# Attention beside a feed-forward network: values multiplied in bursts of four to six key tiles, with some scores copied from PSUM to SBUF

## The chip, the cores and the metric

The kernel runs on one core of one Trainium2 chip. The metric is device time in microseconds of one execution. The kernel before takes 1437.24 us (median of three runs, 1437.2 to 1437.76). TensorE multiplies matrices, ScalarE applies functions, VectorE does elementwise work and copies, GpSimd does some elementwise work and issues transfers, SyncE issues transfers. Matmul results go to PSUM, which has eight banks of 512 float32 columns over 128 partitions; everything else lies in SBUF.

## The reference

```python
def _A_ref(x, wqkv, wo):                     # 2048 tokens, D = 512, 32 heads of 16
    qkv = (x @ wqkv).reshape(B, S, 3, H, Dh) # then (2, 0, 3, 1, 4)
    q, k, v = qkv[0], qkv[1], qkv[2]
    scores = jnp.einsum("bhqd,bhkd->bhqk", q, k) * Dh ** -0.5
    o = jnp.einsum("bhqk,bhkd->bhqd", softmax(scores), v)
    return o.transpose(0, 2, 1, 3).reshape(B, S, D) @ wo

def _B_ref(x, w_gate, w_up, w_down):         # F = 1792
    return (silu(x @ w_gate) * (x @ w_up)) @ w_down

xn = layernorm(A_x)
out = A_x + _A_ref(xn, wqkv, wo) * silu(_B_ref(xn, w_gate, w_up, w_down))
```

All inputs and the output are float32. There is no causal mask: each query meets all 2048 keys.

## The kernel before

**Stages.** A first stage, to about 160 us, normalises the tokens, projects queries, keys and values, and writes them to DRAM, split in a high and a low part of a reduced float32 (each product is made of three: high by high, high by low, low by high). A second, long stage computes attention and mixes the feed-forward network into it, matmul by matmul, on TensorE. A short end projects the last block of queries.

**Attention.** A unit is a group of four heads and a block of 512 queries: `units` = 32, numbered group by group, four blocks `b` to a group `g`. The keys of a unit are 16 key tiles of 128. For each key tile the four heads' scores are four matmuls (`score<-qst,kst`, L811) with 50 contraction rows each; two heads lie on the lower and two on the upper half of the array's rows (`HALF` = 64), so that two heads' scores run side by side. A pair `j` of heads fills `score[j]`, two PSUM banks; ScalarE takes the exp of both at once into an SBUF tile `pr` (128 x 1024, L813). The values (`acc<-pr,vst`, L356) multiply these probabilities by the four heads' values and a column of ones, each head on its own 32 columns of the array, accumulating over the 16 key tiles in the bank `acc[u % 2]`. `finish` then transposes the accumulator on VectorE, divides by the sum of the probabilities, and, at every second group, transposes once more and stores the result to `o_d`.

**Steps.** A step is two key tiles, so there are 256 (`steps` = 8 to a unit). In each, TensorE runs the scores of the first key tile, the values of the step before (`values(prev)`), the scores of the second tile, and then a share of feed-forward matmuls. The two accumulators let a unit's values start while the previous one is being read.

**Feed-forward.** `ffn(b)` is a generator that yields after each pair of matmuls. A pair is two matmuls with 64 contraction rows each, on the two halves of the array's rows, into `bankx` and `banky` (`both`, L174). For each of the 14 tiles of 128 hidden columns there are 24 pairs for gate and up; ScalarE's tanh (L203) and two steps on VectorE make the gated tile, and `split_hidden` and `split_wd` split it and its rows of `w_down` into two parts (`hh`, `wd`). The hidden tiles are in two groups of `GROUPS`, eight and six; after a group, each of the four token tiles takes 3 pairs a hidden tile for the product with `w_down`. The weights of the next tile are split on VectorE by `split_gu` (L134, L135) when a tile begins. After the feed-forward, `project_out` projects the attention's output for the finished blocks of queries.

**Order.** The order on every engine is that of the program text. `plan` lists how many pairs each step takes, `fill` draws them from the generators, `catch_up` runs what was deferred, `out_steps` loads and splits the parts for the output projection as steps pass. SyncE issues most loads in that order, GpSimd stores `o_d`, `g_d` and the output.

**PSUM.** `bankx` and `banky`, two accumulators `acc`, and two score tiles of two banks each: eight banks.

Of the kernel before, what the change touches and what calls it, by code (L numbers as in the profile page):

```python
# [9 lines left out]
F32 = mybir.dt.float32  # L10
# [9 lines left out]
P = 128  # L20
S = 2048
D = 512
H = 32
DH = 16
# [8 lines left out]
GROUPS = (slice(0, 8), slice(8, NF))  # L33
FG = 8
# [7 lines left out]
FIRST = (4, 5, 2, 2)  # L42
HALVED = 2
EARLY = 2
EPS = 1e-5
QSLOT = (0, 1, 0)
# [4 lines left out]
def tile_block(ctx: ExitStack, tc: tile.TileContext, x, wqkv, wo, w_gate, w_up, w_down, out):  # L51
# [78 lines left out]
    def split_gu(i):  # L130
        raw = gu[i][0]
        hi = two.tile([P, DC, P], F32R, tag="guh", name="guh")
        lo = two.tile([P, DC, P], F32R, tag="gul", name="gul")
        dve.tensor_copy(hi, raw)  # L134
        dve.tensor_sub(lo, raw, hi.bitcast(F32))  # L135
        gu[i] = (hi, lo)

# [33 lines left out]

    def both(lhs, rhs, start, stop):
        for bank, h in zip(banks, halves):
            mm(bank, lhs[h], rhs[h], start=start, stop=stop)  # L174
# [8 lines left out]
    def ffn(b):  # L183
        for grp, part in enumerate(GROUPS):
            nf = part.stop - part.start
            for f in range(nf):
                i = b * NF + part.start + f
                if i + 1 < NB * NF:
                    split_gu(i + 1)
# [4 lines left out]
                for c in range(DC):  # L194
                    for wt, j in ((hi, 0), (hi, 1), (lo, 0)):
                        both(wt[:, c], fx[:, j, c], n == 0, n == 3 * DC - 1)
                        n += 1
                        if n == DC and i:
                            load_wd(i)
# [80 lines left out]
    def load_gates(t):  # L280
        gt[t] = (hh, wd)[t % NT // 2].rearrange("p f j t -> p (f j) t")[:, 14 + t % 2].bitcast(F32)
        xr[t] = plain[t % NT]
        sp.dma_start(gt[t], g_d[rows[t]])
        sp.dma_start(xr[t], x[rows[t]])

    stage = {}
    ready = [0] * NB
    splits = []

    def out_steps():  # L290
        for b in range(NB - 1):
            if b not in stage and (len(queue) <= NB, 0 in stage and now > stage.get(0, now), ready[0] == DT)[b]:
                for c in range(DT - 1):
                    load_out(b, c)
                stage[b] = now
            if b in stage and b < 2 and (b, 1) not in stage and now > (u0 + b) * steps:
                load_out(b, DT - 1)
                stage[b, 1] = now
            if b in stage and (b, 2) not in stage and now > stage[b] and (b < 2 or len(queue) <= 2):
                splits.extend((b, c) for c in range(DT - 1))  # L300
                stage[b, 2] = now
                for t in range(0 if b else NT):
                    load_gates(t)
            if (b, 1) in stage and (b, 5) not in stage and now > stage[b, 1]:
                splits.insert(0 if not b else len(splits), (b, DT - 1))
                stage[b, 5] = now
        for _ in range(min(2, len(splits))):
            b, c = splits.pop(0)
            split_o(lhs[b, c], parts_o[b, c])
            ready[b] += 1  # L310

    def store_out(t, y):
        pool.tensor_mul(y, y, gt[t])
        pool.tensor_add(xr[t], y, xr[t])
        (pool if t < end - 1 else sp).dma_start(out[rows[t]], xr[t])
# [34 lines left out]
    def values(item):  # L350
        u, kp, probs = item
        v, a = vst[(u // NB * NB + kp * 2 // CT) % RING], acc[u % 2]
        for i in range(2):
            kt = 2 * kp + i
            for h in range(4):
                mm(a[h * 32:h * 32 + DH + 1], v[:, kt % CT, h * (DH + 1):(h + 1) * (DH + 1)],  # L356
                   probs[2 * i + h // 2][:, h % 2], start=kt == 0, stop=kt == KT - 1, skip_group_check=True)

    def normalise(u, first, last, between=None):
# [3 lines left out]
        dve.transpose(o1[:, :n], acc[u % 2][:, first:last])  # L363
# [8 lines left out]
    def finish(u):  # L372
        g, b = divmod(u, NB)
        normalise(u, 0, TB)
        if g % 2:
            o2 = late.tile([P, TB], F32, tag="o2", name="o2")
            dve.transpose(o2, on[b])  # L377
            if g < NG - 1 or b < 2:
                (pool if g < NG - 1 else sp).dma_start(o_d[g // 2, b], o2)  # L379
            else:  # L380
                whole = hh.rearrange("p f j t -> p (f j) t")
# [6 lines left out]
    steps = KT // 2  # L388

    u0 = units - NB + 1  # L390

# [19 lines left out]


    shares = []

    def plan():
        def tile_of(n, parts):
            shares.extend([n // parts] * parts)

        halved = 0
        for i in range(2 * NB):  # L420
            nf = GROUPS[i % 2].stop - GROUPS[i % 2].start
            for f in range(nf - (i == 0)):
                tile_of(3 * DC, 3 if i or f else 2)
            for t in range(NT):
                if nf == FG:
                    halved += HALVED
                    tile_of(3 * nf, 3 - halved // (NB * NT))
                    halved %= NB * NT
                else:
                    tile_of(3 * nf, 2)  # L430
        for _ in range(EARLY):
            tile_of(3 * (DT - 1), 1)
        for _ in range(NB * NT - NT):
            tile_of(3 * DT, 1)
        shares[0] += 2 - sum(FIRST[:3])
        shares[1] -= 2 + FIRST[3]

# [3 lines left out]
    def share():  # L441
        if not blocked() and shares:
            fill(shares.pop(0))


    with ExitStack() as pro:
# [211 lines left out]
        for b in range(NB):  # L658
# [3 lines left out]
            for n, (make, i) in enumerate(slots):  # L662
# [11 lines left out]
                if not more and n == 2:  # L674
                    split_gu(0)
# [100 lines left out]
    ppool = ctx.enter_context(tc.tile_pool(name="ppool", bufs=6))  # L776
# [5 lines left out]
    score = [spool.tile([P, 2, 512], F32, name=f"score{i}") for i in range(2)]  # L782
    ring(2, RING, att)
# [9 lines left out]
    plan()  # L793
    prev = None

    exps = []
    for u in range(units):
        g, b = divmod(u, NB)
        q = qst[u % 2]
        for kp in range(steps):  # L800
            now = u * steps + kp
            probs = []
            for i in range(2):
                kt = 2 * kp + i
                k, kc = kst[(g * NB + kt // CT) % RING], kt % CT
                if now == i == 0:
                    fill(FIRST[0])
                for j in range(2):
                    for h in range(2):
                        r = slice(h * HALF, h * HALF + NROW)  # L810
                        mm(score[j][:, h], k[r, j, kc * P:(kc + 1) * P], q[r, j], start=True, stop=True)  # L811
                    pr = ppool.tile([P, 2, TB], F32, tag="pr", name="pr")
                    exps.append(act(pr, score[j], AF.Exp, scale=0.25))  # L813
                    if i == 0 and j == 1 and now:
                        tc.add_manual_dep(exps[-1].ins, exps[-3].ins.name, settled, reason="order of the slots' writes")
                    probs.append(pr)
                    if now == i == 0 and j:
                        fill(FIRST[1])
                    elif (now, i, j) in ((0, 1, 0), (1, 0, 0)):
                        fill(FIRST[2 + now])  # L820
                if i == 0:
                    catch_up()
                if i == 0 and prev:
                    values(prev)
            old, prev = prev, (u, kp, probs)
            share()
            if old and old[1] == steps - 1:
                after.append(partial(finish, old[0]))
            if kp == 0:
                if u + 1 < units:  # L830
# [89 lines left out]
```

## Time and profile before

| | us |
|---|---|
| median of three runs | 1437.24 |
| lowest and highest run | 1437.2, 1437.76 |
| span of the profiled execution | 1435.2 |
| TensorE busy | 1427.3 (99%) |
| ScalarE busy | 1111.2 (77%) |
| VectorE busy | 537.9 (37%) |
| GpSimd busy | 90.9 (6%) |

The span runs from the first to the last instruction of one profiled execution; the median of the runs is 2.0 us above it. The page cuts the span into 40 slices and gives the busy tenths of each engine, and the clock that TensorE was granted. Its chain of waits follows the work that ended last back from the end, naming at each step the engine and line. Its groups list, for each line, engine and operation, the written and read tiles, the shapes and count, then the time in which any of them ran, the mean duration of one in nanoseconds, and the idle time of the engine before them with what ended it. A timeline gives start, duration, engine, line, operation and tiles; `PEld` is TensorE's loading of weights, DVE is VectorE, ACT ScalarE and POOL GpSimd. Matmuls overlap in the array, so their pace is read from one start to the next and not from a duration.

### The profile page before, as it was taken

The numbers are of one execution on the slowest core, as the hardware profiler recorded it, in microseconds if no ns is written. First come the engines' busy times: TensorE is split into PE (matmuls) and PEld (weight loads), VectorE is DVE, ScalarE is ACT, GpSimd is POOL, SyncE is SP. The second block draws the span as 40 slices with busy tenths as digits, with TensorE's granted clock in tenths as the row PEclk, the third lists the DMA queues.
The fourth block names the chain that finished last, engine by engine and source line by source line (L and its number), as shares of the span: only waits on it lengthen the run. The fifth ranks groups of instructions, "written<-read, shape, count | busy, mean of one in ns | idle before, by whom it ended". The sixth has DMA issues, their size and how long they took to land.

```text
span 1435.2 us, 26816 instructions
## 1 busy us (share of the span) xinstructions
PE 1427.3 (99%) x11227; PEld 804.0 (56%) x11227; DVE 537.9 (37%) x899; ACT 1111.2 (77%) x1235; POOL 90.9 (6%) x104
## 2 busy tenths in 40 slices
PE   9999999999999999999999999999999999999998
PEld 7778655555555555555555555555555555555555
DVE  6543344112523343134323441243244422243665
ACT  6733688888888888778888888888888887888764
POOL 4200200000000000000000000000000000000154
PEclk9999999999999999999999999999999999999999
DMA  7778652032264321142553320342835210312553
GB/s 222 264 246 248 160 116 63 19 90 65 67 149 120 96 65 34 39 105 71 112 132 90 95 48 12 79 106 55 177 79 123 63 42 12 101 30 78 196 183 104
DMA packets 127524, 149.15 MB, mean 104 GB/s; under 512 B 12588, under 2 KB 79404, under 8 KB 126628
## 3 DMA queue, kind: packets, MB, share of 16 engines
q1 hardware_dynamic: 122196, 126.84, 34.5%
q0 software_dynamic: 4912, 20.12, 3.8%
q8 instruction: 91, 1.49, 0.5%
q10 hardware_dynamic: 288, 0.39, 0.1%
q14 instruction: 37, 0.30, 0.1%
HBM read 107.20 MB, written 40.11 MB: 103 GB/s over the span
## 4 chain that ended last, share of the span: by engine, by line
PE 89%; DVE 0%; DVEq 0%; issue 0%
PE acc L356 33%; PE bankx L174 31%; PE score L811 20%; PE banky L174 3%; PE acc L858 0%; PE banky L858 0%; PE score L858 0%; DVE y L865 0%; DVE y L871 0%; DVEq L916 0%
## 5 line engine op out<-in xcount | busy, mean ns | idle before, releaser
L813 ACT ACTIVATE pr<-score 128x1024 f32<-128x1024 f32 x1024 | 993.2, 1023 | 223.2 <-PE score L811 222.5
L356 PE MATMUL acc<-pr,vst 128*17 128x512 f32 x4096 | 489.2, 595 | 0.0
L811 PE MATMUL score<-qst,kst 50*128 50x512 f32 x2048 | 352.3, 421 | 0.0
L811 PEld LDWEIGHTS score<-qst,kst 50*128 50x128 f32 x2048 | 177.2, 184 | 263.8 <-ACT pr L813 227.9
L174 PE MATMUL bankx<-fx,guh 64*128 64x512 f32 x896 | 288.8, 392 | 0.1
L174 PE MATMUL banky<-fx,guh 64*128 64x512 f32 x896 | 288.7, 392 | 0.0
L356 PEld LDWEIGHTS acc<-pr,vst 128*17 128x17 f32 x4096 | 93.9, 96 | 234.4 <-issue 233.6
L204 DVE SCALAR_TENSOR_TENSOR ga<-th,bankx 128x512 f32<-128x512 f32 x56 | 38.5, 687 | 446.1 <-ACT th L203 446.1
L174 PEld LDWEIGHTS bankx<-fx,guh 64*128 64x128 f32 x896 | 165.7, 185 | 32.8 <-issue 0.9
L174 PE MATMUL banky<-fx,gul 64*128 64x512 f32 x448 | 175.3, 391 | 0.0
L174 PE MATMUL bankx<-fx,gul 64*128 64x512 f32 x448 | 175.3, 391 | 0.0
L174 PEld LDWEIGHTS banky<-fx,guh 64*128 64x128 f32 x896 | 165.6, 185 | 4.0
L174 PE MATMUL bankx<-wd,hh 64*128 64x512 f32 x672 | 166.7, 389 | 0.0
L174 PE MATMUL banky<-wd,hh 64*128 64x512 f32 x672 | 166.6, 388 | 0.0
L174 PEld LDWEIGHTS bankx<-wd,hh 64*128 64x128 f32 x672 | 124.0, 185 | 26.6
L174 PEld LDWEIGHTS banky<-wd,hh 64*128 64x128 f32 x672 | 124.0, 185 | 1.2
L174 PEld LDWEIGHTS bankx<-fx,gul 64*128 64x128 f32 x448 | 82.8, 185 | 17.0
L174 PEld LDWEIGHTS banky<-fx,gul 64*128 64x128 f32 x448 | 82.8, 185 | 2.0
L569 PE MATMUL ps<-xt,wh 128*128 128x512 f32 x256 | 80.6, 396 | 0.0
L222 DVE COPY facc<-bankx 128x512 f32<-128x512 f32 x16 | 11.1, 691 | 171.5 <-PE banky L174 171.5
L135 DVE TENSOR_TENSOR gul<-gur,guh 128x1024 fp32r<-128x1024 f32 x56 | 68.6, 1225 | 2.4 <-DVE guh L134 0.5
L379 POOL DMA_DIRECT2D o_d<-o x12 | 6.5, 545 | 756.5 <-DVE o L377 563.8
(158 smaller groups left out, 1060.5 us busy)
## 6 DMA issues: line engine op xcount, KB each, us to landing
gur<-in_B_w_gate_dram SPq DMA_DIRECT2D x56, 256.0 KB
gur<-in_B_w_up_dram SPq DMA_DIRECT2D x56, 256.0 KB
wdr<-in_B_w_down_dram SPq DMA_DIRECT2D x56, 256.0 KB
kst<-k_d SPq DMA_DIRECT2D x192, 64.0 KB
qst<-q_d SPq DMA_DIRECT2D x192, 64.0 KB
fx<-xt_d SPq DMA_DIRECT2D x24, 512.0 KB
q_d<-parts SPq DMA_DIRECT2D x16, 512.0 KB
k_d<-parts SPq DMA_DIRECT2D x16, 512.0 KB
```

The costliest lines, as they stand in the source:

```text
L135: dve.tensor_sub(lo, raw, hi.bitcast(F32))
L174: mm(bank, lhs[h], rhs[h], start=start, stop=stop)
L204: dve.scalar_tensor_tensor(ga, th, 1.0, bankx, op0=ALU.add, op1=ALU.mult)
L222: dve.tensor_copy(facc[:, t], bankx)
L356: mm(a[h * 32:h * 32 + DH + 1], v[:, kt % CT, h * (DH + 1):(h + 1) * (DH + 1)], probs[2 * i + h // 2][:, h % 2], start=kt == 0, stop=kt == ...
L379: (pool if g < NG - 1 else sp).dma_start(o_d[g // 2, b], o2)
L569: mm(ps, w, a[:, c], start=n == 0, stop=n == 3 * DT - 1)
L811: mm(score[j][:, h], k[r, j, kc * P:(kc + 1) * P], q[r, j], start=True, stop=True)
L813: exps.append(act(pr, score[j], AF.Exp, scale=0.25))
```

## The change

The unit's 16 key tiles are cut into blocks instead of steps. Most units have three blocks, of five, five and six key tiles (`blocks`, with the six where the feed-forward tile is largest); unit 28 has six, six and four; the units in `FINE` (27, 29, 30, 31) have four blocks of four. There are 100 blocks. Each takes one tile of the feed-forward or of the output projection: the list `sizes` holds 24 pairs for a gate and up tile, 21 for a token tile (both groups now have seven hidden tiles), 9 and 12 for tiles of the output projection. All values of a block follow its scores in one burst.

Only `acc[0]` accumulates; `acc[1]` becomes `spare_bank`. A tile of scores (two heads of one key tile) is taken in one of two ways. A direct one (`D`) goes to a score tile of two banks and through ScalarE's exp, as before. A copied one is written head by head into the spare bank (`A` and `B`), each copied by VectorE into half a `pr` tile, and ScalarE's exp over both halves follows in place after the block's other work. A single head takes one half of the array's rows; the other half goes to a feed-forward matmul, for which the order of the halves is swapped while `lower` is set. `events` lays out the order: how many tiles are direct, and where `D`, `A`, `B` and the pairs `F` stand.

```diff
-GROUPS = (slice(0, 8), slice(8, NF))
-FG = 8
+GROUPS = (slice(0, 7), slice(7, NF))
+FG = 7
...
+PROBS = 11
+FINE = (27, 29, 30, 31)
...
-        dve.tensor_copy(hi, raw)
-        dve.tensor_sub(lo, raw, hi.bitcast(F32))
         gu[i] = (hi, lo)
+        for h in (slice(0, DC // 2), slice(DC // 2, DC)):
+            dve.tensor_copy(hi[:, h], raw[:, h])
+            yield
+            dve.tensor_sub(lo[:, h], raw[:, h], hi[:, h].bitcast(F32))
+            yield
...
+    def order():
+        return (1, 0) if lower else (0, 1)
+
     def both(lhs, rhs, start, stop):
-        for bank, h in zip(banks, halves):
-            mm(bank, lhs[h], rhs[h], start=start, stop=stop)
+        for i in order():
+            mm(banks[i], lhs[halves[i]], rhs[halves[i]], start=start, stop=stop)
...
+                        if n % 4 == 2:
+                            next(pieces, None)
...
+    def out_steps():
+        if now == early:
+            for c in range(DT - 1):
+                load_out(0, c)
+        if now == early + 1:
+            for c in range(DT - 1):
+                load_out(1, c)
+            for t in range(NT):
+                load_gates(t)
...
+    def out_splits():
+        if now in (early, early + 1):
+            split_out(now - early)
+        if now == opened[units - 2] + 1:
+            split_out(2)
...
+    def events(n, f):
+        length = 2 * n + f
+        copied = max(0, 2 * n - max(2, (4 * length - 6) // 16 + 1)) if f else 0
+        direct = 2 * n - copied
+        gap = max(4, min(5, (length - 8) / max(1, direct - 2)))
+        marks = [(0, "D"), (1, "D")] + [(7 + gap * i, "D") for i in range(direct - 2)]
+        marks += [(4 + (length - 6) * i / (2 * copied), "AB"[i % 2]) for i in range(2 * copied)]
...
-    ppool = ctx.enter_context(tc.tile_pool(name="ppool", bufs=6))
+    ppool = ctx.enter_context(tc.tile_pool(name="ppool", bufs=PROBS))
...
+            elif e == "D":
+                kt, j = straight[done]
+                for h in order():
+                    scores(score[done % 2][:, h], kt, j, h)
+                probs[kt, j] = ppool.tile([P, 2, TB], F32, tag="pr", name="pr")
+                act(probs[kt, j], score[done % 2], AF.Exp, scale=0.25)
+                done += 1
+                if done == 2:
+                    while ends:
+                        ends.pop(0)()
+                    out_steps()
+            elif e == "A":
+                kt, j = copies.pop(0)
+                waiting.append((kt, j))
+                scores(spare_bank, kt, j, 0)
+                lower = True
+                probs[kt, j] = ppool.tile([P, 2, TB], F32, tag="pr", name="pr")
+                dve.tensor_copy(probs[kt, j][:, 0], spare_bank)
+            else:
+                kt, j = waiting[-1]
+                scores(spare_bank, kt, j, 1)
+                lower = False
+                dve.tensor_copy(probs[kt, j][:, 1], spare_bank)
+        for kt, j in waiting:
+            act(probs[kt, j], probs[kt, j], AF.Exp, scale=0.25)
+        out_splits()
+        catch_up()
+        values(u, range(first, first + n), probs)
```

The layouts that follow from it, by kind of block (key tiles, pairs: number of blocks, direct tiles, copied tiles):

| block | blocks | direct | copied |
|---|---|---|---|
| 4, 9 | 2 | 4 | 4 |
| 4, 12 | 11 | 5 | 3 |
| 4, 21 | 2 | 7 | 1 |
| 4, 24 | 2 | 8 | 0 |
| 5, 21 | 23 | 8 | 2 |
| 5, 24 | 31 | 9 | 1 |
| 6, 21 | 7 | 8 | 4 |
| 6, 24 | 22 | 9 | 3 |

`finish` of a unit is called after the second direct tile of the next unit's first block. `split_gu` yields between its four operations, and one of them is drawn at every fourth pair. The loads of keys, values, output parts and gates move from steps to blocks. The last twelve pairs of the output projection come after the last values. The scratch for GpSimd's transfers is set to 4096 bytes.

214 lines of the change are left out of this document (99 added, 115 removed).

## The prediction

> **What bounds the kernel now.** I read the page first, then the busy time of the attention stretch, then the timeline of single instructions.
>
> ```profile
> span 1435.2 us, 26816 instructions
> ...
> PE   9999999999999999999999999999999999999998
> ...
> PEclk9999999999999999999999999999999999999999
> ...
> PE acc L356 33%; PE bankx L174 31%; PE score L811 20%; PE banky L174 3%; PE acc L858 0%; PE banky L858 0%; PE score L858 0%; DVE y L865 0%; DVE y L871 0%; DVEq L916 0%
> ...
> L813 ACT ACTIVATE pr<-score 128x1024 f32<-128x1024 f32 x1024 | 993.2, 1023 | 223.2 <-PE score L811 222.5
> L356 PE MATMUL acc<-pr,vst 128*17 128x512 f32 x4096 | 489.2, 595 | 0.0
> L811 PE MATMUL score<-qst,kst 50*128 50x512 f32 x2048 | 352.3, 421 | 0.0
> ...
> L135 DVE TENSOR_TENSOR gul<-gur,guh 128x1024 fp32r<-128x1024 f32 x56 | 68.6, 1225 | 2.4 <-DVE guh L134 0.5
> L222 DVE COPY facc<-bankx 128x512 f32<-128x512 f32 x16 | 11.1, 691 | 171.5 <-PE banky L174 171.5
> ```
> ```profile
> 160.00:1420.00 1260.00, 1260.00 (x10430) 673.86 (x10432) 452.36 (x698) 1028.93 (x1096) 58.79 (x66) 1.00 0.35 87
> ```
>
> The second fence is the stretch 160 to 1420 us: length, then busy time of TensorE, its weight loads, VectorE, ScalarE, GpSimd, and the granted clock, 1.00. TensorE is never idle in it, so the end is set by TensorE's pace alone, and any wait put in front of a matmul is added to the time in full. How much of the pace is lost between kinds of matmul is seen in one step:
>
> ```profile
> 704.22 0.39 PE L174 MATMUL bankx<-wd,hh 64*128 64x512 f32 x1
> ...
> 704.45 0.39 PE L174 MATMUL bankx<-wd,hh 64*128 64x512 f32 x1
> ...
> 706.04 0.63 PE L811 MATMUL score<-qst,kst 50*128 50x512 f32 x4
> 706.50 1.94 ACT L813 ACTIVATE pr<-score 128x1024 f32<-128x1024 f32 x2 [0.64 <-PE score L811]
> ...
> 706.60 1.91 PE L356 MATMUL acc<-pr,vst 128*17 128x512 f32 x16
> 707.04 0.12 PEld L356 LDWEIGHTS acc<-pr,vst 128*17 128x17 f32 x4 [0.31 <-issue]
> 707.47 0.12 PEld L356 LDWEIGHTS acc<-pr,vst 128*17 128x17 f32 x4 [0.31 <-issue]
> ...
> 708.44 0.73 PE L811 MATMUL score<-qst,kst 50*128 50x512 f32 x4
> ...
> 709.00 0.40 PE L174 MATMUL bankx<-wd,hh 64*128 64x512 f32 x1
> ```
>
> A feed-forward pair takes a slot of 0.23 us (704.22 to 704.45), and so should a pair of scores. Four scores (two pairs, 0.46) take 0.56 from 706.04 to 706.60, and 0.56 from 708.44 to 709.00: 0.10 is lost on each side of a values burst. Inside, four quads by 0.43 (707.04 to 707.47) are 1.71, but the burst holds TensorE for 1.84 (706.60 to 708.44): 0.13 more. A burst costs 0.33 us beside its work.
>
> **The change, part by part.** *Fewer bursts.* 4096 records at 16 a burst are 256 bursts. The changed code cuts the 32 units into 28 of three blocks and 4 of four, 100 bursts. The work inside (slots, quads) is the same. 156 x 0.33 = 51 us off. I take it whole; its lower bound is nothing, if the loss came back at the new borders between scores and feed-forward, but runs of 4 scores that border on feed-forward pairs show no loss on that side.
>
> *What ScalarE now paces.* Two exps take 1.94 and one 1.02, so one starts each 0.92 us. Direct tiles are written 4 slots apart, 0.92: no stall, no slack. In a block of five key tiles with 24 pairs, TensorE takes 34 x 0.23 + 0.33 + 10 x 0.43 = 12.4 us, ScalarE 10 x 0.92 + 0.60 = 9.8. Not the bound.
>
> *Scores copied through one bank.* The other tiles' scores go one head at a time into the single bank acc[1], VectorE copies them out, and the next head's matmul waits for that copy, with all TensorE work behind it. The cycle is matmul to copy, copy, copy to matmul:
>
> ```profile
> 710.84 0.39 PE L174 MATMUL banky<-wd,hh 64*128 64x512 f32 x1
> ...
> 711.26 0.69 DVE L226 TENSOR_TENSOR y<-bankx,facc 128x512 f32<-128x512 f32 x1 [5.73 <-PE banky L174]
> ```
> ```profile
> 42.06 0.69 DVE L552 TENSOR_TENSOR xt<-acc,xt 128x512 fp32r<-128x512 f32 x1 [0.54 <-ACT xt L549]
> ...
> 42.80 0.31 PEld L544 LDWEIGHTS acc<-ident,xn 128*128 128x128 f32 x3 [0.56 <-DVE xt L552]
> ```
>
> 0.42 (710.84 to 711.26) + 0.69 (the copy, 691 ns of L222) + 0.05 (42.75 to 42.80) = 1.16. If a weight load must run after the release, its 0.18 makes 1.34. I take 1.22, near the lower end, as the load is pulled ahead elsewhere. The Trainium skill (Perfetto Trace Analysis, Optimizing Tensor Performance) says that independent matmul groups should rotate through several banks, so that one's evacuation overlaps the next's matmuls; one bank goes against it. By that rule the copies would hide with a second bank, and the term below would be nothing; here there is one.
>
> The code spaces a block's copies evenly, whatever VectorE needs. Worked for four key tiles with 12 pairs (six copies, 2.33 slots = 0.54 us apart): the first head is written 1.03 us into the block (four slots and the 0.11 after a burst), the sixth no sooner than 1.03 + 5 x 1.22 = 7.13, and three and a half slots follow: 7.93, against 20 x 0.23 + 0.11 = 4.71 unhindered, so 3.2 us lost. By the same sum:
> - four tiles, 12 pairs: 11 blocks x 3.2 = 35;
> - four tiles, 9 pairs (eight copies): 2 x 6.1 = 12;
> - six tiles, 21 pairs (eight copies, 0.78 apart): 7 x 2.9 = 20;
> - six tiles, 24 pairs (six copies, 1.15 apart, VectorE also splitting weights between them, 1225 / 2 ns a piece against the 0.5 us free per cycle): 22 x 0.65 = 14;
> - five tiles: copies 1.4 us or more apart, nothing.
> Together 81. The gaps between copies are 11 x 5 + 2 x 7 + 7 x 7 + 22 x 5 = 228; 0.06 less or 0.12 more each gives 67 to 108.
>
> *Eleven probability buffers, twelve tiles.* In a block of six the last direct exp takes the buffer of the block's first tile, so it waits for the first quad of the values; the tanh (24 pairs only) and the copied exps queue behind it on ScalarE.
>
> ```profile
> 799.61 0.60 ACT L203 ACTIVATE th<-bankx 128x512 f32<-128x512 f32 x1
> 800.10 1.94 ACT L813 ACTIVATE pr<-score 128x1024 f32<-128x1024 f32 x2
> ```
>
> A tanh holds ScalarE for 0.49 (799.61 to 800.10). Counted from the values' start, with 0.6 for the quad and the handoff: 0.6 + 0.92 + 0.49 + 2 x 0.92 + 1.02 + 0.1 = 5.0 until the last copied exp can be read, and 0.6 + 4 x 0.92 + 1.02 + 0.1 = 5.4 with 21 pairs. The sixth key tile is due after ten quads, 4.3, or its second half after eleven, 4.7; which, the rows do not tell. I take the middle, 0.5 and 0.9: 22 x 0.5 + 7 x 0.9 = 17 us; 0 if other slack exists, 24 with the earlier due time.
>
> *VectorE's queue at a unit's start.* The accumulator's transposition, which was done beside a step, now stands ahead of the block's first copy:
>
> ```profile
> 800.24 0.69 DVE L204 SCALAR_TENSOR_TENSOR ga<-th,bankx 128x512 f32<-128x512 f32 x1 [6.85 <-ACT th L203]
> ...
> 803.28 0.69 DVE L145 TENSOR_TENSOR wd<-wdr,wd 128x512 fp32r<-128x512 f32 x1
> ...
> 814.76 0.69 DVE L204 SCALAR_TENSOR_TENSOR ga<-th,bankx 128x512 f32<-128x512 f32 x1 [8.93 <-ACT th L203]
> ```
> ```profile
> 1382.67 1.65 DVE L262 TENSOR_TENSOR hh<-hh 128x512 fp32r<-128x512 f32 x1
> 1384.25 0.70 DVE L363 STREAM_TRANSPOSE o<-acc 128x512 f32<-128x512 f32 x1
> ...
> 1385.79 0.71 DVE L377 STREAM_TRANSPOSE o<-on 128x512 f32<-128x512 f32 x1
> ...
> 1387.00 0.69 DVE L262 TENSOR_TENSOR hh<-o,hh 128x512 fp32r<-128x512 f32 x1
> ```
>
> It takes 1.5 us (1384.25 to 1385.79), 2.3 with the second transposition, 3.4 with the split for the output projection; and a tile's 3.7 us of gating and splitting (800.24 to 803.97) begins after its tanh and reaches about 1 us into the next block. A block's first copy would start at 1.03 + 0.42 = 1.45; where it starts later and copies are the chain, the difference is lost. Units 30 and 31: 0.3 + 3.4 - 1.45 = 2.3 each. Unit 29, where three splits of an output part also stand in the queue (2 us of them left over): 4.3, and 0.6 in each of two later blocks. Two six-tile blocks at a unit's start: 1.5 each. Five-tile blocks there, five with 21 pairs by about 1.4 and seven with 24 by 0.4: 10. The splits of `wo` and of the last output parts before unit 29: 3.5. About 27 us; 8 to 45, the upper end with L262 at 1.65, as at 1382.67 beside GpSimd.
>
> *The rest.* The tail gains a leftover output tile (12 pairs) after the last values, whose two VectorE steps of 0.69 and 0.42 of latency now stand ahead of the last transposition: 2 us. Exps of copied scores read SBUF; no such exp is shown, nearest is
>
> ```profile
> L645 ACT CAST fx<-xt 64x1024 fp32r<-64x1024 f32 x16 | 16.8, 1048 | 0.3
> DVE wd L144 <- DMA wdr<-in_B_w_down_dram: 10.4, 2, 6.4
> ```
>
> at 1048 against 1023, nothing on the path. The moved loads (keys, gates, output parts on SyncE; stores on GpSimd) are hidden now: VectorE waited for a weight tile twice in all. A tile came each 14.5 us (800.24 to 814.76), it now comes each 12 to 14, so they stay hidden; 0, at most 3. The smaller scratch for GpSimd's transfers has no row: 0 to 2, taken as 0, since TensorE waits for none of them.
>
> Sum: -51 + 81 + 17 + 27 + 2 = +76. On the profiled execution's 1435.2 that is 1511; the runs' median, 1437.24, lies 2.0 above that span, so **1513**.
>
> **The rivals.** *VectorE keeps up* and the copies hide, as the even spacing supposes: 1437 - 51 + 2 = 1388, faster. For it: VectorE was busy 452 of 1260 us, and 428 copies add 296. Against: latency, not load, decides. It holds as soon as the copy cycle is below the spacing, 0.54 us in the last 11 blocks; the rows give 1.16.
>
> *Only the cycle stalls*, in the blocks that have no slack, and buffers and queue cost nothing: 1437 - 51 + 81 + 2 = 1469. For it: the order within a quad and slack on ScalarE are not seen in the trace.
>
> *The switches remain*: the change doesn't remove what it says, the 0.33 reappears where single heads are mixed in, and the stalls come on top: 1513 + 51 = 1564. Against it: pairs on opposite row halves run at 0.23 now.
>
> *The clock falls.* The trace has TensorE at 1.00 and never idle here, so it cannot show what short gaps do. Should the 20 blocks with the densest copies (9, 12 and six tiles with 21 pairs: 11 x 8.3 + 2 x 7.6 + 7 x 12.9, about 200 us of TensorE work by the rows above) run at half clock, a supposition, and half of the loss hide behind the copies, it is 1513 + 100 = 1613. The Trainium skill (TensorE: Matmul & The Clock Gate, A second HAM failure mode: psum-queue depth-cycling) reports such an oscillation where TensorE idles briefly between groups.
>
> *The terms cancel*: 1437, if stalls come to 51.
>
> **How the numbers follow.** Forecast 0.66, VectorE keeps up 0.07, only the cycle 0.13, switches remain 0.08, clock 0.03, cancel 0.03. The likeliest's own range, with each term at its ends, is -51 + 67 + 0 + 8 + 2 = +26 to -51 + 108 + 24 + 45 + 7 = +133, so 1463 to 1570; not all ends come together. For 8 in 10 I take 1455 to 1570. Runs here agree within 0.04%; a change of under 0.2%, 3 us, is none. Faster 0.08 (keeps up, and a little of cancel), same 0.04, slower 0.88.
>
> **What would show it.** TensorE's idle time before scores into acc put down to VectorE's copies, 60 to 110 us, in the blocks of 9, 12 and 21 pairs; starts of such scores 1.2 us apart in the last 110 us; 100 values bursts; waits of values for ScalarE only in six-tile blocks; a last stretch of 13 blocks at about 11.5 us each. I am wrong if heads are written closer than 1.1 us apart, or if feed-forward pairs between them stretch beyond 0.23.

## The result, and the profile after

The changed kernel takes 1583.45 us (median of four runs, 1582.48 to 1586.93) where the kernel before took 1437.33 beside it (1437.2 to 1437.76). The ratio is 1.102, with a 95% interval of 1.1006 to 1.1035. It is slower, as forecast, but by 146 us instead of 76, and the time lies above the forecast range.

These are lines of the page of the changed kernel: span, tenths of TensorE's busy time and of its granted clock in 40 slices, the chain by engine and by line, and groups (line, engine, operation, tiles, shapes, count; busy us and mean ns of one; idle us before them and its end).

```profile
span 1581.4 us, 27925 instructions
...
PE   9999799999999999999999999999999999888887
...
PEclk9999899999999999999999999999999999877978
...
PE 85%; DVE 8%; ACT 4%; issue 2%; DMA 1%; SPq 0%; DVEq 0%; ACTq 0%
PE acc L370 29%; PE bankx L182 18%; PE score L835 12%; PE banky L182 9%; PE acc L835 7%; PE ps L591 5%; ACT pr L846 3%; DVE pr L858 3%; PE ps L593 3%; DVE pr L863 1%; DVE o L377 1%; ACT pr L865 0%; DVE o L391 0%; PE acc L566 0%; DMA v_d<-vt 0%
...
L858 DVE COPY pr<-acc 128x512 f32<-128x512 f32 x214 | 147.6, 690 | 206.0 <-PE acc L835 193.6
...
L835 PE MATMUL acc<-qst,kst 50*128 50x512 f32 x428 | 200.0, 467 | 52.0 <-DVE pr L858 32.8
...
L865 ACT ACTIVATE pr<-pr 128x1024 f32<-128x1024 f32 x214 | 214.5, 1060 | 0.0
```

Before, no engine but TensorE had a share above 0% in the chain of waits. Now VectorE holds 8% of it and ScalarE 4%. TensorE has two weak places, slice 5 and the last six slices, and the granted clock falls in both. L858 and L863 are VectorE's copies of the two heads, 0.69 us each as forecast. Summed by what was waited for (us, times, longest), the weight loads of copied scores and of values, and ScalarE's exps, say whom they waited for:

```profile
PEld acc L835 <- DVE pr L858: 64.8, 77, 3.0
PEld acc L370 <- ACT pr L865: 59.9, 83, 0.8
PEld acc L835 <- DVE pr L863: 46.2, 92, 1.1
```
```profile
ACT pr L846 <- PE acc L370: 56.8, 29, 2.8
```

The copies hold the scores' weight loads back for 111 us (64.8 + 46.2). In 29 cases an exp of direct scores waits for the values: there are exactly 29 blocks of six key tiles, and it is their twelfth probability tile that waits for a buffer. An engine's wait is not yet TensorE's loss, however; for that each block is measured on TensorE. Two blocks of four key tiles and 12 pairs ran at full clock from end to end; one of them has splits of an output part in VectorE's queue ahead of its copies. Here is the other, first TensorE (without the feed-forward matmuls), then VectorE:

```profile
1492.23 0.74 PE L835 MATMUL score<-qst,kst 50*128 50x512 f32 x4
1493.27 0.39 PE L835 MATMUL acc<-qst,kst 50*128 50x512 f32 x1
1494.52 0.49 PE L835 MATMUL acc<-qst,kst 50*128 50x512 f32 x1 [0.38 <-DVE pr L858]
...
1495.80 0.50 PE L835 MATMUL acc<-qst,kst 50*128 50x512 f32 x1 [0.32 <-DVE pr L863]
...
1499.78 0.49 PE L835 MATMUL acc<-qst,kst 50*128 50x512 f32 x1 [0.40 <-DVE pr L858]
1500.91 3.63 PE L370 MATMUL acc<-pr,vst 128*17 128x512 f32 x32
1504.46 0.50 PE L835 MATMUL score<-qst,kst 50*128 50x512 f32 x2
```
```profile
1493.77 0.69 DVE L858 COPY pr<-acc 128x512 f32<-128x512 f32 x1 [3.60 <-PE acc L835]
1495.05 0.69 DVE L863 COPY pr<-acc 128x512 f32<-128x512 f32 x1 [0.59 <-PE acc L835]
1496.40 0.69 DVE L858 COPY pr<-acc 128x512 f32<-128x512 f32 x1 [0.66 <-ACT pr L846]
```

One cycle through the bank: matmul at 1494.52, copy at 1495.05, its end at 1495.74, next matmul at 1495.80, so 0.53 + 0.69 + 0.06 = 1.28 us. Over the block's six heads, from 1493.27 to 1499.78, the mean distance is 1.30. From first score to first value the block takes 1500.91 - 1492.23 = 8.68 us. Its 20 slots of 0.23 and 0.20 for the borders are 4.80, so 3.88 is lost. The 3.55 of the values are the 8 x 0.428 + 0.115 of a burst without waits.

The same subtraction over all 100 blocks, by kind, beside what the prediction gave each place (copies' cycle + VectorE's queue where there are two; its two six-tile blocks at a unit's start are taken as those of units 9 and 20, with 24 pairs):

| place | blocks | forecast, us | measured, us |
|---|---|---|---|
| first two blocks, scores and pairs | 2 | 0, at most 3 | 16.9 |
| six key tiles, values burst | 29 | 17 | 40.0 |
| six key tiles, 21 pairs, scores and pairs | 7 | 20 | 27.5 |
| six key tiles, 24 pairs, scores and pairs | 21 | 14 + 3 | 16.5 |
| five key tiles | 53 | 10 | 15.9 |
| four key tiles, 12 pairs, all | 11 | 35 + 6 | 66.0 |
| four key tiles, 9 pairs, all | 2 | 12 + 8 | 23.3 |
| four key tiles, 21 or 24 pairs | 4 | 0 | 0.7 |
| sum | | 125 | 206.8 |

The attention stretch lasts from 160.1 to 1564.4 us instead of 159.9 to 1422.8, 141.4 more, and the tail 17.0 instead of 12.4, 4.6 more. Together that is the 146. Without the 206.8 the stretch would be 1197.5, 65 less than before, where 51 was forecast. The leftover output tile that moved behind it is 2.8 of these 14; the rest was not separated.

The row nobody had forecast is the first. These are VectorE's operations in block 0, from its timeline, then the scores behind them on TensorE:

```profile
166.15 1.24 DVE L169 CAST hh<-ga 128x512 fp32r<-128x512 f32 x1 [10.28 <-DMA v_d<-vt]
...
170.37 0.69 DVE L858 COPY pr<-acc 128x512 f32<-128x512 f32 x1
...
171.20 0.76 PE L835 MATMUL acc<-qst,kst 50*128 50x512 f32 x1 [5.48 <-DVE pr L858]
```
```profile
187.27 0.43 DVE L147 CAST wd<-wdr 128x512 fp32r<-128x512 f32 x1 [7.22 <-DMA wdr<-in_B_w_down_dram]
...
188.68 0.69 DVE L858 COPY pr<-acc 128x512 f32<-128x512 f32 x1
```

VectorE stands 10.28 us for transfers of the first stage, in block 1 7.22 us for a weight tile. Waits of this length existed before, but no TensorE work depended on what was queued behind them. Now a copy does, and TensorE stands for 5.48 us until it is done.

The clock, in the busy times by stretch (length, then busy us of TensorE, weight loads, VectorE, ScalarE, GpSimd, then the granted clock):

```profile
160.00:190.00 30.00, 18.36 (x129) 12.46 (x131) 12.08 (x19) 13.61 (x15) 6.35 (x6) 0.82 0.67 152
190.00:1369.00 1179.00, 1168.35 (x9385) 677.44 (x9383) 629.93 (x1065) 901.27 (x978) 15.10 (x28) 1.00 0.32 77
1369.00:1564.00 195.00, 165.15 (x919) 69.53 (x916) 100.72 (x151) 101.49 (x104) 35.13 (x33) 0.81 0.22 71
```

In the last stretch the mean is 0.81. The record has only 1.0 and 0.5, so some 195 x 0.19 x 2 = 74 us of it were at half clock.

### The profile page after: what moved, and what is told of

It is laid out like the page before. It is cut to its first block, busy times and chain, and to the rows that moved or that the text cites. A ratio compares the mean times of both kernels' runs of the same rounds, so it can differ in the third digit from the quotient of the medians.

```text
span 1581.4 us, 27925 instructions
## 1 busy us (share of the span) xinstructions
PE 1520.2 (96%) x11227; PEld 890.6 (56%) x11227; DVE 829.0 (52%) x1439; ACT 1098.2 (69%) x1235; POOL 89.4 (6%) x104
## 4 chain that ended last, share of the span: by engine, by line
PE 85%; DVE 8%; ACT 4%; issue 2%; DMA 1%; SPq 0%; DVEq 0%; ACTq 0%
PE acc L370 29%; PE bankx L182 18%; PE score L835 12%; PE banky L182 9%; PE acc L835 7%; PE ps L591 5%; ACT pr L846 3%; DVE pr L858 3%; PE ps L593 3%; DVE pr L863 1%; DVE o L377 1%; ACT pr L865 0%; DVE o L391 0%; PE acc L566 0%; DMA v_d<-vt 0%
## 5 line engine op out<-in xcount | busy, mean ns | idle before, releaser
L846 ACT ACTIVATE pr<-score 128x1024 f32<-128x1024 f32 x810 | 778.7, 1027 | 384.6 <-PE score L835 322.4
L835 PE MATMUL score<-qst,kst 50*128 50x512 f32 x1620 | 411.3, 419 | 0.0
L182 PE MATMUL banky<-fx,guh 64*128 64x512 f32 x896 | 319.8, 399 | 0.0
L182 PE MATMUL bankx<-fx,guh 64*128 64x512 f32 x896 | 312.3, 395 | 0.1
L858 DVE COPY pr<-acc 128x512 f32<-128x512 f32 x214 | 147.6, 690 | 206.0 <-PE acc L835 193.6
L835 PE MATMUL acc<-qst,kst 50*128 50x512 f32 x428 | 200.0, 467 | 52.0 <-DVE pr L858 32.8
L863 DVE COPY pr<-acc 128x512 f32<-128x512 f32 x214 | 148.0, 692 | 139.2 <-PE acc L835 135.4
L865 ACT ACTIVATE pr<-pr 128x1024 f32<-128x1024 f32 x214 | 214.5, 1060 | 0.0
L182 PE MATMUL bankx<-wd,hh 64*128 64x512 f32 x672 | 205.8, 395 | 0.0
L182 PE MATMUL banky<-wd,hh 64*128 64x512 f32 x672 | 196.5, 394 | 0.0
L835 PEld LDWEIGHTS acc<-qst,kst 50*128 50x128 f32 x428 | 81.4, 190 | 131.3 <-DVE pr L858 64.8
```

The source lines that it names most:

```text
L182: mm(banks[i], lhs[halves[i]], rhs[halves[i]], start=start, stop=stop)
L835: mm(bank, k[r, j, kc * P:(kc + 1) * P], q[r, j], start=True, stop=True)
L846: act(probs[kt, j], score[done % 2], AF.Exp, scale=0.25)
L858: dve.tensor_copy(probs[kt, j][:, 0], spare_bank)
L863: dve.tensor_copy(probs[kt, j][:, 1], spare_bank)
L865: act(probs[kt, j], probs[kt, j], AF.Exp, scale=0.25)
```

## The experiments

**One part of the change mended at a time.** Each of the next four runs, and the one with filled gaps, is a single execution; the four of the change spread over 4.4 us. *No copies in the first two blocks:*

```diff
-        copied = max(0, 2 * n - max(2, (4 * length - 6) // 16 + 1)) if f else 0
+        copied = max(0, 2 * n - max(2, (4 * length - 6) // 16 + 1)) if f and now > 1 else 0
```

> The change with no copied scores in its first two blocks (all their tiles go direct); all else as changed. In the changed kernel's trace these two blocks hold their scores and pairs for 8.2 and 8.6 us longer than the unhindered sum, beside VectorE waiting 10.3 and 7.2 us for transfers. Theory (the copies stand behind VectorE's waits for transfers, and TensorE behind the copies): both blocks lose at most 2 us, the clock is 1.00 until the last output tiles; 1583 - 15 = 1568 (1564 to 1572). Rival (the late weights and keys themselves hold TensorE): 1580 to 1586.

1569.45 us, 14 less. VectorE still stands for the same transfer,

```profile
165.41 1.24 DVE L169 CAST hh<-ga 128x512 fp32r<-128x512 f32 x1 [9.78 <-DMA v_d<-vt]
```

but the two blocks lose 1.9 and 2.2 us instead of 8.3 and 8.6, although VectorE's wait for the weight tile grew from 7.2 to 12.4. It is the copy behind the waiting instruction that costs, not the wait.

*Twelve buffers instead of eleven* (room for it from a shared tile and a smaller scratch):

```diff
-PROBS = 11
+PROBS = 12
...
-            o2 = late.tile([P, TB], F32, tag="o2", name="o2")
+            o2 = late.tile([P, TB], F32, tag="o1", name="o2")
...
-dynamic_dma_scratch_size=4096)
+dynamic_dma_scratch_size=2048)
```

> The change with twelve probability buffers instead of eleven (room from half the transfer scratch and one shared late tile). Theory (in blocks of six the last direct exp waits for the first values, and the copied exps queue behind it): the values of those 29 blocks lose their 1.3 to 1.7 us each, 40 us in all; 1583 - 40 = 1543 (1538 to 1552). Rival (ScalarE has too much to do in such a block whatever the buffers): 1575 to 1586, values still 1.0 us or more late.

1546.79 us, 37 less. The bursts of six key tiles lose 0.03 to 0.05 us each, where they lost 1.27 (24 pairs) and 1.72 (21 pairs). ScalarE's 29 waits for the values are gone from the summed waits, and of the values' waits for copied exps there remain

```profile
PEld acc L370 <- ACT pr L865: 17.4, 53, 0.7
```

instead of 59.9. Of these, 13.7 us in 44 waits of at most 0.31 are still in the six-tile blocks with 24 pairs, where they cost nearly nothing (0.03 to 0.05 us a block): a weight load that waits is not yet a matmul that waits. The values of the four-tile blocks of 9 and 12 pairs still lose 12 us.

*A copy of 64 columns instead of 512*, into a scratch tile. The exps of copied scores read the block's first direct probabilities, so copied scores do not enter the output:

```diff
-                dve.tensor_copy(probs[kt, j][:, 0], spare_bank)
+                dve.tensor_copy(short, spare_bank[:, :64])
...
-            act(probs[kt, j], probs[kt, j], AF.Exp, scale=0.25)
+            act(probs[kt, j], probs[straight[0]], AF.Exp, scale=0.25)
```

> The change with VectorE reading only 64 of the 512 columns of each copied head, into a scratch tile; the exps of copied tiles read a direct tile's probabilities instead, so that the copied scores do not count in the result. Number and order of instructions and waits between TensorE and VectorE stay. Theory (the cycle through one bank sets the pace): it falls from 1.28 to 0.42 + 0.2 + 0.05 = about 0.7, the blocks of 9, 12 and 21 pairs lose 1 us instead of 3.5 to 11, the clock stays at 1.00 there; 1583 - 100 = 1480 (1465 to 1495), with the values' waits of 40 us and the start left. Rival (the mixing of single heads with pairs, or ScalarE, sets the pace): 1550 or more.

1455.23 us. The matmuls, exps and copies are as many as in the change, only the copies shorter (0.22 instead of 0.69 us), and 128 us go. Four of the copies (shortest, middle and longest in ns, first and last start, shape):

```profile
L859 DVE COPY short<-acc x4: 224/224/226, 271.0 to 284.1; 128x64 f32<-128x64 f32 x4
```

The blocks with six key tiles and 21 pairs lose 0.6 us instead of 3.9 before their values, and those with 12 pairs 2.0 instead of 5.2 in the mean (an ordinary one, neither at a unit's start nor behind a split, 1.3 instead of 4.7); two heads in a row stand 0.81 apart in the last blocks. Over all blocks the losses before the values fall by 84 us. It went 25 us further than expected, since the edit does more than shorten copies: exps no longer wait for them, and ScalarE's 29 waits for the values are gone, so that the bursts of six key tiles lose nothing either, though there are still eleven buffers. Why the buffer comes free in this run the trace does not say. So the copy's length is the root of most of the loss before the values; for the rest this run is no clean test, and it does not separate cycle, buffers and clock.

*At most one copied tile where a block has 9 or 12 pairs:*

```diff
+        if f <= 12:
+            copied = min(copied, 1)
```

> The change with at most one copied tile in the 13 blocks of 9 and 12 pairs, instead of four and three; the others go direct, paced by ScalarE. Theory (the dense copies cost there, and the clock falls because TensorE stands still): these blocks' scores and pairs take 5.7 us instead of 9.5 to 15, their values 3.6, and the clock stays at 1.00 in them: 1583 - 65 = 1518 (1508 to 1530). Rival (the clock falls there for the tail's own sake, or ScalarE is the bound): 1560 or more, clock below 0.98.

1527.38 us, 56 less. An ordinary block of 12 pairs loses 1.3 us instead of 4.7. The three blocks at a unit's start and one behind a split of an output part still lose 2.9 to 4.6, with a single copied tile in each: the queue in front of the copy, most likely, as it is what sets them apart.

**The clock.** The scores of direct tiles, from the third of a block on, are multiplied four times into the same banks, in blocks of 9 and 12 pairs alone, so that TensorE works in the gaps:

```diff
-                for h in order():
-                    scores(score[done % 2][:, h], kt, j, h)
+                for _ in range(4 if f <= 12 and done >= 2 else 1):
+                    for h in order():
+                        scores(score[done % 2][:, h], kt, j, h)
```

> The change with every direct tile from the third on, in the blocks of 9 and 12 pairs, multiplied four times instead of once into the same banks: 37 tiles at 0.7 us more matmul each, 25 us of TensorE work, put where it stands still. Theory (the clock falls because TensorE stands still between copies, and the fall costs 1 to 1.5 us of each such block's 13.7): the halved stretches after 1369 us shrink from 79 us to under 40, and the time falls by 5 to 20 us, to 1565 to 1578, for all the added work. Rival (the clock follows something else, or its fall hides behind the copies): 1583 to 1608.

1577.27 us: some 25 us more work for TensorE (37 tiles x 3 pairs x 0.23), and 6 us less time. The granted clock of the last stretch rises from 0.81 to

```profile
1369.00:1558.00 189.00, 169.47 (x1144) 92.45 (x1140) 100.18 (x151) 101.89 (x104) 35.04 (x33) 0.89 0.22 73
```

and of the nine blocks of 12 pairs that do not open a unit eight lose 3.86 to 3.88 us before their values, the figure of the change's block shown above (the ninth is behind a split). After 1369 us there are 45 us at half clock instead of 80, not under 40 as expected; those nine blocks have none left, where they had seven stretches. In the change the nine average 4.7. So the added work fits into the gaps, and the stalled stretch is paced by the copies; the clock adds some 0.8 us a block. The blocks of 9 pairs and the units' starts, where TensorE is idle for 1.3 to 2.6 us at a time, still fall to half clock, so the clock's full price is not separated by this run.

**All of it together.** Twelve buffers; no copies in the first two blocks, nor at a unit's start or behind a split with 9 or 12 pairs; one copied tile in other such blocks, two at most elsewhere:

```diff
+MOST = {(4, 9): 1, (4, 12): 1}
...
-    def events(n, f):
+    def events(n, f, quiet):
...
+        copied = 0 if now < 2 or f <= 12 and quiet else min(copied, MOST.get((n, f), 2))
...
-        direct, todo = events(n, f)
+        direct, todo = events(n, f, first == 0 or now in (early + 2, opened[units - 2] + 2))
```

> The change with all four losses mended: no copies in the first two blocks, twelve buffers, at most two copied tiles a block and one in the blocks of 9 and 12 pairs (none in such blocks at a unit's start and in two behind the splits). Theory (these four and nothing else ate the 51 us of fewer bursts): 1584 - 14 (start) - 40 (values' waits) - 30 (six-tile blocks) - 60 (last blocks) = 1440 (1428 to 1452), clock above 0.99. Rival (bursts or single heads beside pairs cost something not yet seen): 1465 or more.

1441.84 us against 1437.55, ratio 1.0031 (1.0018 to 1.0043). Of the 146 us, 142 are gone, but the 51 of the fewer bursts have not come in. The attention ends at 1421.1, 1.7 earlier than before, and by the subtraction used above its blocks still lose 63 us. The waits name ScalarE, in the lines of the matmuls and of the weight loads:

```profile
PE score L837 <- ACT pr L848: 16.6, 43, 0.8
```
```profile
PEld score L837 <- ACT pr L848: 71.4, 231, 1.1
```

Scores now wait for ScalarE. The matmuls' line is the one that counts: before the change no score stood in it, while the weight loads' line had 227.9 us without any idle time of TensorE in the attention stretch. Of the 16.6 us, 11.8 are in the blocks of 9 and 12 pairs, which lose 24 of the 63; what the other 39 are was not separated. Every tile that is not copied must pass one of two score tiles and an exp; with nearly all direct, a block of four key tiles shows them 0.92 apart:

```profile
1345.83 0.50 PE L837 MATMUL score<-qst,kst 50*128 50x512 f32 x2 [0.38 <-ACT pr L848]
1346.74 0.50 PE L837 MATMUL score<-qst,kst 50*128 50x512 f32 x2 [0.41 <-ACT pr L848]
1347.66 0.50 PE L837 MATMUL score<-qst,kst 50*128 50x512 f32 x2 [0.42 <-ACT pr L848]
1348.33 3.63 PE L371 MATMUL acc<-pr,vst 128*17 128x512 f32 x32
```

No scores are made while the values run for 3.6 us, and before them ScalarE is what TensorE waits for in this block. Fewer and longer bursts bunch the exps there; the copies were to cover that, and cost more than it.

*Two copied tiles in the blocks of 12 pairs, otherwise the same:*

```diff
-MOST = {(4, 9): 1, (4, 12): 1}
+MOST = {(4, 9): 1, (4, 12): 2}
```

> As the one before, with two copied tiles instead of one in the seven later blocks of 12 pairs that copy at all. Theory: four heads through one bank take 1.03 + 3 x 1.28 and 0.6, 5.5 us, against 6.1 measured with one copied tile, paced by ScalarE: 4 us less, 1436 (1426 to 1450). Rival (one bank is already the longer way with four heads): 2 to 8 us more.

1449.24 us (ratio 1.0083, 1.0066 to 1.0099), 7 more than with one: the gain that was expected from more copies is a miss. Ordinary blocks lose 1.7 us before the values and 0.55 in them, against 1.3 and 0.02 with one. *Three copied tiles with 21 pairs* were tried on top of the next kernel:

```diff
-MOST = {(4, 9): 1, (4, 12): 1}
+MOST = {(4, 9): 1, (4, 12): 1, (6, 21): 3}
```

> As the steps in the tail, with three copied tiles instead of two in the seven blocks of six key tiles and 21 pairs. If their remaining 1.2 us each is ScalarE's pace over ten direct tiles, it goes to about 0.6: 4 us less than the steps in the tail. If the cycle through one bank decides (six heads 1.28 apart fit into 7.7 of 7.8 us, but VectorE's other work comes in between), it is 3 to 10 us more.

1442.23 us, 2.7 more than the kernel it was built on (1439.49): the seven blocks lose 1.7 us each instead of 1.2. The difference in time is little above the spread of the runs (1437.88 to 1441.15 there, 1441.01 to 1444.36 here). In both places more relief for ScalarE by way of VectorE makes it worse.

**A version that beats both?** The three last units go back to steps of two key tiles, all scores direct, the values of the step before in between, six or seven pairs to a step:

```diff
+            for j in range(2):
+                for h in range(2):
+                    r = slice(h * HALF, h * HALF + NROW)
+                    mm(score[j][:, h], k[r, j, kc * P:(kc + 1) * P], q[r, j], start=True, stop=True)
+                probs[kt, j] = ppool.tile([P, 2, TB], F32, tag="pr", name="pr")
+                act(probs[kt, j], score[j], AF.Exp, scale=0.25)
+            if kt % 2 == 0:
+                catch_up()
+                if held:
+                    values(*held.pop())
...
+            else:
+                fill(shares.pop(0))
+                held.append((u, (kt - 1, kt), probs))
...
+    shares = [9] + [6] * 16 + [7] * 6 + [6]
```

> As all mended, but the last three units go back to steps of two key tiles (scores of one key tile, the values of the step before, scores of the other, then six or seven pairs), in 24 steps, all scores direct, and the leftover output tile is shared among them. If all copies of these units cost more than the bursts there save, as the theory has it, the 12 blocks that took 1299.6 to 1421.1 in 'all mended' become 24 steps of (4 + 6.4) x 0.23 + 4 x 0.43 + 0.33 = 4.4 us, 107 us, and the tail is about 4 us shorter: 1442 - 14 - 4 = 1424, faster than before (1437.5). Rival: ScalarE (four exps of 0.92 to a step, 3.7) and the single accumulator stall the steps as well, and the time stays at 1435 to 1445.

1439.49 us against 1437.52 (ratio 1.0014, 1.0004 to 1.0024), so a miss: the rival was right. Its timeline, feed-forward matmuls left out:

```profile
1363.36 0.39 PE L832 MATMUL score<-qst,kst 50*128 50x512 f32 x2
1364.00 0.49 PE L832 MATMUL score<-qst,kst 50*128 50x512 f32 x2 [0.24 <-ACT pr L834]
1364.42 1.91 PE L371 MATMUL acc<-pr,vst 128*17 128x512 f32 x16
...
1368.22 0.39 PE L832 MATMUL score<-qst,kst 50*128 50x512 f32 x2
1368.86 0.50 PE L832 MATMUL score<-qst,kst 50*128 50x512 f32 x2 [0.25 <-ACT pr L834]
1369.29 1.91 PE L371 MATMUL acc<-pr,vst 128*17 128x512 f32 x16
```

From values to values it takes 4.87 us (1364.42 to 1369.29), where the scores, six pairs, values and borders come to 10 x 0.23 + 4 x 0.43 + 0.33 = 4.35: the second tile's two exps (2 x 0.92) must end before the next scores, and those stand before the next values. With 12 pairs to a step, as before the change, this chain is hidden; with six it is not.

So in 14 of the 24 steps one of the four tiles is copied through the spare bank, its heads six places apart in the order, and the direct ones are spread (`D` direct, `A` and `B` copied heads, `F` pairs, `V` values; the first order is for steps at a unit's start or behind splits):

```diff
+        for e in "DDVDDFFFFFFFFF" if quiet else "DAFFDFFBFDFFFFFV":
```

> As the steps in the tail, but 14 of their 24 steps copy one of the four tiles of scores through the spare bank (its heads seven slots, 1.6 us, apart) and spread the three direct ones, with the values last. The trace of the steps in the tail has a step at 4.86 us, with the chain exp, exp, scores, values, scores longer than TensorE's 4.4 to 4.6. If this chain is what held those steps, 14 of them get 0.3 to 0.45 shorter: 1439.5 - 5 = 1434.5, below the time before. If the copies stall TensorE as in the change (over 0.4 us a step), the time is 1440 to 1446.

1434.61 us (11 runs) against 1437.15, ratio 0.9987 (0.9978 to 0.9996). Its median lies below both kernels', below the one before by 0.04 to 0.22%, no more than its own runs spread (1434.53 to 1437.87). One step without and one with copies:

```profile
1355.61 1.91 PE L371 MATMUL acc<-pr,vst 128*17 128x512 f32 x16
...
1360.48 1.91 PE L371 MATMUL acc<-pr,vst 128*17 128x512 f32 x16
...
1366.87 1.91 PE L371 MATMUL acc<-pr,vst 128*17 128x512 f32 x16
...
1369.05 0.39 PE L833 MATMUL acc<-qst,kst 50*128 50x512 f32 x1
...
1370.29 0.50 PE L833 MATMUL acc<-qst,kst 50*128 50x512 f32 x1
...
1371.43 1.05 PE L371 MATMUL acc<-pr,vst 128*17 128x512 f32 x8
```

4.87 without (1355.61 to 1360.48), 4.56 with (1366.87 to 1371.43). The two heads stand 1.24 us apart (1369.05 to 1370.29), not the 1.6 that were expected: just one cycle, and TensorE has other work until the bank is free; no wait for a copy is left in front of the copied scores of these steps. So the copying works with two heads a step that leave each other one whole cycle.

## Why the prediction was right and wrong

- *The direction, and what decides it*, held: the latency of matmul, copy, matmul through one bank, not VectorE's load. The forecast cycle was 1.22 us, the measured one 1.28: the copy starts 0.53 after the matmul, not 0.42, while copy (0.69) and release (0.06) came out as read. The choice of 1.22 rested on a weight load that is pulled ahead. It was not: behind a copy the load, 0.18, begins with its matmul (both at 1497.15 in the block shown), and that matmul takes 0.50 where the block's first head, which waits for nothing, took 0.39. The mean distance is 1.30, so five gaps make 0.4 of the 0.7 us by which an ordinary block of 12 pairs, at full clock, exceeded its 3.2 (3.88); the other 0.3 is behind the last head (1.13 instead of 0.80 until the values). The cycle's term of 81 was some 15 us too small (0.7 x 11 here, 7.5 in the row of six key tiles and 21 pairs).
- *Fewer bursts, -51*: a five-tile block that does not open a unit loses 0.2 to 0.5 us, 15.9 in all with the queue (10 forecast), and the rest of the stretch gained 65 where 51 stood. The switches did not come back; that rival is out.
- *Eleven buffers, 0.5 and 0.9 us a block*: the mechanism was right (29 waits, and they vanish with a twelfth buffer), the size not. Measured were 1.27 and 1.72. The middle between two ends was taken, and even the upper end, 24 us in all (its own rows give 23), is below the measured 40. The first step of the sum shows why. Block 1 of the change, its values' start and the exp that waits for the buffer:

```profile
197.87 6.59 PE L370 MATMUL acc<-pr,vst 128*17 128x512 f32 x48
...
199.02 1.02 ACT L846 ACTIVATE pr<-score 128x1024 f32<-128x1024 f32 x1 [1.76 <-PE acc L370]
```

  The exp starts 1.15 us after the values, where 0.6 was taken for quad and handoff: 0.55 of the 0.77 that a block with 24 pairs lost beyond its 0.5.
- *VectorE's queue at a unit's start, 27*: right in kind, too small in the last units. The starts of units 30 and 31 lose 7.9 and 7.3 us before the values, where an ordinary block loses 4.7 and the queue's part was put at 2.3: about 3 instead, some of it at half clock. The two six-tile blocks at a unit's start lost 0.8 more than others of their kind, not 1.5.
- *"The moved loads ... stay hidden; 0, at most 3"* is the step whose mechanism failed. It showed two waits of VectorE's for a weight tile, 10.4 us together, and took them for hidden because TensorE waited for neither. A third stands in the waits of before and was left out:

```profile
DVE hh L166 <- DMA v_d<-vt: 10.7, 1, 10.7
```

  It did not ask what would be queued behind such a wait once VectorE's copies feed TensorE. This one and one for a weight tile cost 16.9 us in the first two blocks; without copies there, the time fell by 14, to 1569.45, just inside the range.
- *The clock*, given 0.03 and only as a supposition: it did fall, in the last stretch and at the start, but that was not what made the time. At full clock the ordinary last blocks would lose 3.9 instead of 4.7 us.

Of the 82 us by which the losses exceed their forecast, 23 are the buffers', 17 the start's, 25 the blocks with 12 pairs (18 of them remain in the run with filled gaps, 58.9 against 41), and the remaining 17 are spread over the other kinds. The unhindered part took 14 back, which is luck, since nothing in the sum stood for it, and the tail added 2.6. Of the signs named beforehand, the last 13 blocks took 15.1 us each instead of 11.5, and TensorE's own idle time before copied scores was 43 us (32.8 + 10.3), not 60 to 110; the 111 are its weight loads'.

## What to carry to other kernels

When an engine is drawn into the chain that feeds the bound one, every wait it already has, for a transfer or for its own queue, comes onto the path: list these waits with their lengths, the start included. A copy through a single bank costs its whole round trip, so space the uses of the bank by that, not by the engine's share of busy time; where two heads in a step stood 1.24 us apart the copy paid, where six were set 0.54 apart it cost 4 us a block. And before bunching work to save switches, ask which other engine paces the items in between: here, once most copies were taken away, the blocks still lost 63 us and used up the saving, in the last blocks by scores that waited for exps.

## What the hardware showed

TensorE's clock fell to half in stretches without any long pause. In the second 12-pair block of unit 29, TensorE's idle times are at most 0.39 us, one in each 1.3 us:

```profile
1426.06 0.50 PE L835 MATMUL acc<-qst,kst 50*128 50x512 f32 x1 [0.38 <-DVE pr L858]
...
1428.70 0.79 PE L835 MATMUL acc<-qst,kst 50*128 50x512 f32 x1 [0.39 <-DVE pr L858]
```
```profile
1421.00:1428.00 7.00, 5.59 (x37) 3.18 (x33) 2.81 (x5) 3.98 (x4) 0.59 (x1) 1.00 0.58 188
1428.00:1432.00 4.00, 3.61 (x18) 1.49 (x19) 2.72 (x4) 3.60 (x4) 0.00 (x0) 0.59 0.14 54
```

The matmul's duration goes from 0.50 to 0.79, the clock from 1.00 to 0.59 in the mean of the next 4 us. By starts, TensorE has 2.3 slots of 0.23 to do in each 1.3 us and stands for the rest. The half-clock stretches in the record of the change are 3.4, 6.8, 10.2 and 13.7 us long, multiples of one length, but for one that the end cuts off. Filling the gaps ended all seven in the nine blocks of 12 pairs that do not open a unit; in the blocks of 9 pairs they stayed. The Trainium skill (TensorE: Matmul & The Clock Gate, A second HAM failure mode: psum-queue depth-cycling) describes this of another kernel, short idle times between groups of matmuls that make the clock swing between half and full, and this case agrees (1.00 to 0.59 here). The rule as the same page of the Trainium skill states it (HAM oscillation — how this bites in real kernels), no idle gaps of TensorE above some 3.4 us, would have let these blocks run at full clock; here the measurement, 0.39 us at most, decides against it as a sufficient rule.
